# Scores of a linear-attention chunk: 64-key blocks on the two halves of TensorE, masked by four VectorE instructions instead of one

## The chip, the cores and the metric

The kernel runs on one core of one Trainium2 chip. Times are device microseconds of one execution. A run of a kernel consists of several executions, and the median is given; beside it stands one execution that the hardware profiler recorded, with a time and a span of its own.

## The reference

An attention layer with a complex decay per channel is followed by a gated feed-forward layer. Batch 4, 8 heads, 768 tokens, head dimension 48:

```python
for t in range(S):
    new_re = ar * S_re - ai * S_im
    new_im = ar * S_im + ai * S_re
    kv = np.einsum('bhd,bhe->bhde', k[:, :, t], v[:, :, t])
    S_re, S_im = (new_re + kv, new_im)
    y[:, :, t] = np.einsum('bhd,bhde->bhe', q[:, :, t], S_re)
...
a = x @ w_a
b = x @ w_b
return (a * b @ w_out)
```

`ar` and `ai` are the decay of token t, with its magnitude limited to 0.999; x is y with the heads side by side (384 columns); the feed-forward layer is 1536 wide. All of it is float32.

## The kernel before

The 768 tokens are cut into six chunks of 128. A *unit* is one chunk of two batches; there are 12 units, 0 to 11, in two runs of six (units 0 to 5 for the first two batches, 6 to 11 for the others). Within a chunk the recurrence is written as attention: with P the running product of decays, the queries are multiplied by P and the keys divided by P, real and imaginary parts are stacked to 96 rows, and the output of a token is the sum over the keys of its chunk that are not later than itself, plus what the state from earlier chunks gives.

Four kinds of work run beside each other:

- `prep(u)`: VectorE and ScalarE compute the products P of a unit and multiply queries and keys in place in the tile `qk`. Much of it is VectorE work on 128x768 elements.
- `stack(u)`: DMAs issued on SP copy each head's 96 rows from `qk` into the tile `stk` (128 rows, the last 32 are zero; per head 256 query columns, 256 key columns).
- `attn(u)`: the attention of the unit, 18 pieces (12 in the last chunk of a run). `scores` multiplies keys by queries: for a batch i and four heads `hg`, four matmuls of 128 keys by 128 queries fill one PSUM buffer (`pm`, two of these), and one VectorE instruction multiplies it by a 0/1 mask (a query sees only keys that are not later) into the SBUF tile `am` (two copies, one per `hg`). `transposes` turns the keys around, through a `pm` buffer too; `outputs` multiplies `am` by the values and, from the second chunk on, the queries by the state, on four 32-column strips of TensorE (`tile_position=(0, qd * 32)`) into the tile `xp`; `state` updates the state.
- `gemm1(f)` and `gemm2(f)`: the feed-forward layer of the unit before in 12 slices f. Operands are split into a high and a low part, so each product is three matmuls. `gemm1` leaves its result in a PSUM buffer `ab` (three of these), ScalarE and VectorE turn it into `hh` and `hl`, and `gemm2` runs two slices later (`LAG`).

In the steady state (the loop over `w`), while the feed-forward of unit w runs, the pieces of `attn(w+1)` are put between its slices (from slice 5 or 6 on), VectorE works at `prep(w+3)` in portions between slices, and `stack(w+2)` follows at slice 10 or 11. The order of instructions on each engine is made by a planner from the program's order, priorities and its own costs: `high_priority` puts the feed-forward's evacuation (`MOE_FIRST`, 4000) ahead of the attention's (`ATTN_FIRST`, 2000), and that ahead of `prep`. On the chip each engine then goes through its own list in order. Where a matmul has no `tile_position`, it uses the whole 128x128 array.

The lines that matter below: 385 (the matmuls of the scores), 388 (the mask), 396 (transposes), 425 (outputs), 442 (state), 486 and 504 (the two products of the feed-forward), 494 to 497 (their evacuation).

Of the kernel before, what the change touches and what calls it, by code (L numbers as in the profile page):

```python
# [8 lines left out]
F32 = mybir.dt.float32  # L9
# [5 lines left out]
ALU = mybir.AluOpType  # L15
# [15 lines left out]
NG = NB // RUNS  # L31
# [25 lines left out]
ATTN_FIRST = 2000  # L57
# [4 lines left out]
def view(ap, offset, dims):  # L62
    return bass.AP(tensor=ap.tensor, offset=ap.offset + offset, ap=[list(ap.ap[0])] + dims)


def at_(i):
    return i // 2 * 2 * NB + i % 2
# [3 lines left out]
def tile_kernel(ctx: ExitStack, tc: tile.TileContext, a_d, qk_d, v_d, w_d, qn_d, kn_d, vn_d, an_d, out_d):  # L71
    nc = tc.nc
    vec, act, pe, sync = nc.vector, nc.scalar, nc.tensor, nc.sync

    const = ctx.enter_context(tc.tile_pool(name="const", bufs=1))
# [4 lines left out]
    small = fast.enter_context(tc.tile_pool(name="small", bufs=2))  # L80
    vpool = fast.enter_context(tc.tile_pool(name="vpool", bufs=2))
    kvp = fast.enter_context(tc.tile_pool(name="kvp", bufs=2))
# [6 lines left out]

    ident = const.tile([128, 128], F32, name="ident")  # L90
    make_identity(nc, ident)
    mask = const.tile([128, 128], F32, name="mask")
    nc.gpsimd.memset(mask, 1.0)
    nc.gpsimd.affine_select(out=mask, in_=mask, pattern=[[1, 128]], compare_op=ALU.is_ge,
                            fill=0.0, base=0, channel_multiplier=-1)
    biases = const.tile([128, 6], F32, name="biases")
    b_tiny, b_sq, b_eps, b_one, b_inv, b_rsq = (biases[:, i:i + 1] for i in range(6))
    vec.memset(b_tiny, TINY)
# [10 lines left out]
    stk = const.tile([128, H, RUN], F32, name="stk")  # L109
# [93 lines left out]
    def prep(u):  # L203
# [9 lines left out]
        for k in (1, 0):  # L213
            vec.tensor_tensor(out=view(zz, (1 + k) * W, PAIRS), in0=a_t[:, k].rearrange("p (b i e) -> p b i e", e=2, i=SUB // 2),
                              in1=sc.rearrange("p (b i e) -> p b i e", e=2, i=SUB // 2), op=ALU.mult)
# [7 lines left out]
        def tok(s, i, o, n):  # L223
            return zb[:, s, i // 2, o:o + n, i % 2]

        parts = [(p * NB // 2, NB // 2) for p in range(2)] if u == 0 else [(0, NB)]
        for i in range(1, SUB):
            pr = small.tile([128, 2, 2, NB], F32, name="pr", bufs=1)
            for o, n in parts:
                vec.tensor_tensor(  # L230
                    out=pr[:, :, :, o:o + n],
                    in0=view(zz, W + at_(i) + 2 * o, [[W, 2], [-W, 2], [2, n]]),
                    in1=tok(slice(1, 3), i - 1, o, n).unsqueeze(1).broadcast_to([128, 2, 2, n]),
                    op=ALU.mult)
            for o, n in parts:
                vec.tensor_tensor(out=tok(slice(1, 3), i, o, n), in0=pr[:, :, 0, o:o + n],  # L236
                                  in1=pr[:, :, 1, o:o + n], op=ALU.add)
# [18 lines left out]
        cc, bb = c_t[:], b_t[:]  # L256

        def joined(out, x, y, n):
            pb = small.tile([128, 2, 2, NG], F32, name="pb")
            vec.tensor_tensor(out=pb[:, :, :, 0:n], in0=x,  # L260
                              in1=y.unsqueeze(1).broadcast_to([128, 2, 2, n]), op=ALU.mult)
            vec.tensor_tensor(out=out, in0=pb[:, :, 0, 0:n], in1=pb[:, :, 1, 0:n], op=ALU.add)

        vec.tensor_copy(out=c_t[:, 1:3, 0], in_=view(zz, W + at_(SUB - 1), [[W, 2], [2 * RUNS, NG]]))
        for k in range(1, RUNS):
            joined(c_t[:, 1:3, k], view(zz, W + at_(SUB - 1) + 2 * k, [[W, 2], [-W, 2], [2 * RUNS, NG]]),
                   c_t[:, 1:3, k - 1], NG)
        vec.tensor_scalar(out=c_t[:, 0], in0=c_t[:, 2], scalar1=-1.0, scalar2=None, op0=ALU.mult)
        n_run = NSB // RUNS
        for k in range(n_run):  # L270
            dst = b_t[:, 1:3, :, (k + 1) * RUNS] if k + 1 < n_run else b8
            joined(dst, view(cc, NB + (RUNS - 1) * NG + k, [[NB, 2], [-NB, 2], [n_run, G]]), b_t[:, 1:3, :, k * RUNS], G)
        pr = small.tile([128, 2, 2, RUNS - 1, NG], F32, name="pr", bufs=1)
        for k in range(2):
            vec.tensor_tensor(out=pr[:, k], in0=view(cc, (1 + k) * NB, [[-NB, 2], [NG, RUNS - 1], [1, NG]]),
                              in1=view(bb, NB, [[NB, 2], [0, RUNS - 1], [RUNS, NG]]), op=ALU.mult)
        vec.tensor_tensor(out=view(bb, NB + 1, [[NB, 2], [1, RUNS - 1], [RUNS, NG]]),
                          in0=pr[:, :, 0], in1=pr[:, :, 1], op=ALU.add)
# [10 lines left out]
        for k in range(2):  # L289
            pz = a_t  # L290
            for s in range(2):
                vec.tensor_tensor(  # L292
                    out=pz[:, s].rearrange("p (j b e) -> p j b e", j=SUB // 2, e=2), in0=zb[:, 1 + s],
                    in1=view(bb, (1 + k - s) * NB, [[0, SUB // 2], [1, NB], [0, 2]]), op=ALU.mult)
# [3 lines left out]
                              in0=view(pz[:], 0, PAIRS), in1=view(pz[:], W, PAIRS), op=ALU.add)  # L298
            yield 870
        act.activation(out=a_t, in_=z[:, 0:2], func=AF.Square)  # L300
        if rescaled(c):
            vec.tensor_tensor(out=bn[:, 1:3, :, 0], in0=b8,
                              in1=rho[:].unsqueeze(1).broadcast_to([128, 2, G]), op=ALU.mult)
# [67 lines left out]
    def attn(u, xh, xl):  # L371
# [3 lines left out]
        ams, kts, xps = {}, {}, {}  # L375

        def cols(i):
            return slice(i * C, (i + 1) * C), slice(TOK + i * C, TOK + (i + 1) * C)

        def scores(i, hg):  # L380
            qs, ks = cols(i)
            sp = ps_m.tile([128, 4, 128], F32, name="pm")
            for h4 in range(4):
                h = hg * 4 + h4
                pe.matmul(out=sp[:, h4], lhsT=stk[:, h, ks], rhs=stk[:, h, qs], start=True, stop=True)  # L385
            am = kvp.tile([128, 512], F32, name="am", bufs=2).rearrange("p (h t) -> p h t", h=4)
            with tc.high_priority(offset=ATTN_FIRST):
                vec.tensor_tensor(out=am, in0=sp, in1=mask[:].unsqueeze(1).broadcast_to([128, 4, 128]),  # L388
                                  op=ALU.mult)
            ams[i, hg] = am  # L390

        def transposes(i, hg):
            qs, ks = cols(i)
# [42 lines left out]
        def state(i, hg):  # L436
# [10 lines left out]
            with tc.high_priority(offset=ATTN_FIRST):  # L447
# [4 lines left out]
                if rescaled(c):  # L452
                    vec.tensor_tensor(out=uv, in0=uv, in1=sv, op=ALU.mult)

        order = [(scores, 0, 0), (scores, 0, 1), (transposes, 0, 0), (transposes, 0, 1),
                 (outputs, 0, 0), (outputs, 0, 1), (scores, 1, 0), (residual, 0, 0), (state, 0, 0), (scores, 1, 1),
                 (state, 0, 1), (transposes, 1, 0), (transposes, 1, 1), (outputs, 1, 0),
                 (outputs, 1, 1), (state, 1, 0), (residual, 1, 0), (state, 1, 1)]
        if u == 0:
            order = [(scores, 0, 0), (scores, 0, 1), (outputs, 0, 0), (outputs, 0, 1), (scores, 1, 0), (scores, 1, 1),  # L460
                     (residual, 0, 0), (outputs, 1, 0), (outputs, 1, 1), (transposes, 0, 0), (transposes, 0, 1),
                     (residual, 1, 0), (state, 0, 0), (state, 0, 1), (transposes, 1, 0), (transposes, 1, 1),
                     (state, 1, 0), (state, 1, 1)]
        for fn, i, g in order:
            if not (last and fn in (transposes, state)):
                fn(i, g)
                yield

    def pieces(u):
        return 12 if u % NCH + 1 == NCH else 18  # L470
# [161 lines left out]
    for _ in attn(0, *x_cur):  # L632
        drain(p1, P1_A)
# [13 lines left out]
    for w in range(NU):  # L647
        last = w + 1 == NU
        x_nxt = None if last else new_x()
        at = None if last else attn(w + 1, *x_nxt)  # L650
        if not last:
            load_v(w + 1)
# [13 lines left out]
        for f in range(NF):  # L666
            if w == 0:
                next(ws, None)
                drain(p1, P1_F)
                if f == P1_AT:  # L670
                    drain(p1)
                    stack(1)
                    for i in range(WARM):
                        wp = ps_m.tile([128, 512], F32, name="pm")
                        pe.matmul(out=wp[:, 0:TOK], lhsT=ident, rhs=qk[:, i % NJ, 1 - i // NJ % 2, TOK:2 * TOK],
                                  start=True, stop=True)
# [87 lines left out]
```

## Time and profile before

| | us |
|---|---|
| median of 3 runs | 698.79 (698.2 to 699.16) |
| profiled execution | 698.89 |
| its span | 697.2 |
| TensorE busy (matmuls) | 655.2, 5854 records |
| VectorE busy | 551.8, 1241 instructions |
| ScalarE busy | 308.9 |
| score matmuls, line 385 | 54.4 busy, 384 records |
| mask, line 388 | 32.8 busy, 48 instructions |

Matmul records overlap, since their ends are modelled: the mean duration of a record is not the time that it takes from its successors. A float32 matmul has two records, a matmul of the split feed-forward operands one. The chain of work that ended last, in order of time, merges neighbours of one line into one row (start, length, engine, tile, line, how many), and there the length of a row is what it took of the time.

### The profile page before, as it was taken

To read this page: it belongs to the slowest core of one execution; us is meant where nothing else is said; L and a number is where in the kernel's file an instruction comes from. 1 tells how busy PE (TensorE), PEld (TensorE's weight loads), DVE (VectorE), ACT (ScalarE), POOL (GpSimd) and SP (SyncE) were. 2 spreads that over 40 slices of the span, in tenths; PEclk is the share of its full clock that TensorE was granted. 3 is DMA by queue.
4 is the path that set the end of the run, shared out by engine and by line. 5 is a ranking of instruction groups with operands and counts; after the bars stand their busy time and mean duration, and the time that the engine had idled before them with its cause. 6 is when DMAs were issued, how large, how long until landed. Compare 5 with 4: busy or idle time off the path is not lost.

```text
span 697.2 us, 14316 instructions
## 1 busy us (share of the span) xinstructions
PE 655.2 (94%) x5854; PEld 610.8 (88%) x5854; DVE 551.8 (79%) x1241; ACT 308.9 (44%) x618; POOL 5.6 (1%) x11
## 2 busy tenths in 40 slices
PE   3557999999999999999999999999999999999996
PEld 1224889899899999999999999999999999999996
DVE  5999899988888889989899898999989853232221
ACT  6357755634535445245363554535542332221221
POOL 3000000000000000000000000000000000000000
PEclk9567999999999999999999999999999999999999
DMA  8973202411414205134151340511510500400000
GB/s 312 402 291 108 79 1 54 129 55 55 128 42 130 81 28 149 60 98 129 25 160 46 102 134 1 169 67 47 145 46 2 165 25 17 106 24 2 24 1 28
DMA packets 32088, 63.94 MB, mean 92 GB/s; under 512 B 3984, under 2 KB 10640, under 8 KB 32016
## 3 DMA queue, kind: packets, MB, share of 16 engines
q1 hardware_dynamic: 28560, 58.23, 27.0%
q10 hardware_dynamic: 3456, 4.72, 1.9%
q8 instruction: 48, 0.79, 0.5%
q14 instruction: 24, 0.20, 0.1%
HBM read 39.32 MB, written 4.72 MB: 63 GB/s over the span
## 4 chain that ended last, share of the span: by engine, by line
PE 64%; DVE 27%; ACT 4%; DMA 2%; issue 1%; SPq 1%; ACTq 0%; DVEq 0%
PE ab L486 30%; PE o L504 14%; PE xp L425 6%; PE pm L385 5%; PE pm L442 4%; DVE a_t L292 3%; DVE pr L230 2%; DVE qk L312 2%; DVE h_t L495 2%; PE pm L396 2%; DVE hl L497 2%; PE pm L150 2%; DVE z L297 2%; DVE pb L260 1%; DVE z L236 1%
## 5 line engine op out<-in xcount | busy, mean ns | idle before, releaser
L486 PE MATMUL ab<-xh,w 128*128 128x256 f32 x1728 | 339.0, 285 | 0.0
L486 PEld LDWEIGHTS ab<-xh,w 128*128 128x128 f32 x1728 | 278.1, 190 | 1.8 <-issue 1.4
L486 PE MATMUL ab<-xl,w 128*128 128x256 f32 x864 | 245.1, 284 | 0.0
L486 PEld LDWEIGHTS ab<-xl,w 128*128 128x128 f32 x864 | 164.4, 190 | 0.5 <-issue 0.2
L504 PE MATMUL o<-w,hh 128*128 128x384 f32 x576 | 152.3, 344 | 0.0
L494 ACT COPY h_t<-ab 128x256 f32<-128x256 f32 x144 | 53.1, 369 | 176.9 <-PE ab L486 176.8
L495 DVE TENSOR_TENSOR h_t<-ab,h_t 128x256 f32<-128x256 f32 x144 | 60.5, 420 | 72.5 <-ACT h_t L494 72.3
L504 PEld LDWEIGHTS o<-w,hh 128*128 128x128 f32 x576 | 96.8, 190 | 3.7 <-issue 3.0
L504 PE MATMUL o<-w,hl 128*128 128x384 f32 x288 | 96.9, 336 | 0.0
L496 ACT CAST hh<-h_t 128x256 fp32r<-128x256 f32 x144 | 58.0, 403 | 81.1 <-DVE h_t L495 80.9
L497 DVE TENSOR_TENSOR hl<-h_t,hh 128x256 fp32r<-128x256 f32 x144 | 60.5, 420 | 17.5 <-ACT hh L496 17.3
L150 PE MATMUL ab<-o_sb,ident 128*128 128x384 f32 x42 | 29.1, 794 | 29.9 <-DVE o_sb L141 29.8
L385 PE MATMUL pm<-stk 128*128 128x128 f32 x384 | 54.4, 279 | 2.7 <-DMA stk<-qk 2.7
L504 PEld LDWEIGHTS o<-w,hl 128*128 128x128 f32 x288 | 54.1, 188 | 0.0
L385 PEld LDWEIGHTS pm<-stk 128*128 128x128 f32 x384 | 48.7, 191 | 5.9 <-issue 4.8
L230 DVE TENSOR_TENSOR pr<-z 128x384 f32<-128x384 f32 (+1 forms) x91 | 47.1, 524 | 2.4 <-ACT z L216 0.8
L150 PEld LDWEIGHTS ab<-o_sb,ident 128*128 128x128 f32 x42 | 10.2, 286 | 39.8 <-DVE o_sb L141 29.4
L292 DVE TENSOR_TENSOR a_t<-z,b_t 128x768 f32<-128x768 f32 x48 | 44.6, 952 | 0.1
L425 PE MATMUL xp<-am,v_t 128*32 128x128 f32 x768 | 42.5, 277 | 1.3 <-DVE am L388 1.2
L312 DVE TENSOR_TENSOR qk<-qk,z 128x1536 f32<-128x1536 f32 (+1 forms) x28 | 42.7, 1524 | 0.1
L388 DVE TENSOR_TENSOR am<-pm,mask 128x512 f32<-128x512 f32 x48 | 32.8, 685 | 5.0 <-PE pm L385 4.8
L425 PE MATMUL xp<-stk,u 128*32 128x128 f32 x640 | 34.4, 273 | 0.0
(106 smaller groups left out, 761.7 us busy)
## 6 DMA issues: line engine op xcount, KB each, us to landing
w<-in_dram SPq DMA_DIRECT2D x36, 384.0 KB, 8.1
qk<-in_dram SPq DMA_DIRECT2D x12, 768.0 KB, 4.8
a_t<-in_dram SPq DMA_DIRECT2D x11, 768.0 KB, 4.3
stk<-qk SPq DMA_DIRECT2D x42, 192.0 KB, 3.3
v_t<-in_dram SPq DMA_DIRECT2D x24, 256.0 KB, 2.7
out_dram<-o_sb ACTq DMA_DIRECT2D x24, 192.0 KB, 1.9
stk<-qk SPq DMA_DIRECT2D x18, 192.8 KB, 3.4
stk<-qk SPq DMA_DIRECT2D x14, 128.0 KB, 3.1
```

Source lines behind the costliest of these rows:

```text
L150: pe.matmul(out=lp[:, 0:n], lhsT=ident, rhs=t, start=True, stop=False)
L230: vec.tensor_tensor(out=pr[:, :, :, o:o + n], in0=view(zz, W + at_(i) + 2 * o, [[W, 2], [-W, 2], [2, n]]), in1=tok(slice(1, 3), i - 1, o, ...
L292: vec.tensor_tensor(out=pz[:, s].rearrange("p (j b e) -> p j b e", j=SUB // 2, e=2), in0=zb[:, 1 + s], in1=view(bb, (1 + k - s) * NB, [[0, ...
L312: vec.tensor_tensor(out=qk4[:, :, k, x0:x1], in0=qk4[:, :, 1, x0:x1], in1=z[:, k].rearrange("p (j t) -> p j t", j=NJ).unsqueeze(2).broadca ...
L385: pe.matmul(out=sp[:, h4], lhsT=stk[:, h, ks], rhs=stk[:, h, qs], start=True, stop=True)
L425: pe.matmul(out=xp[qd * 32:(qd + 1) * 32, ti], lhsT=l, rhs=rr, start=st, stop=sp_, tile_position=(0, qd * 32), skip_group_check=True)
L486: pe.matmul(out=ab[:, m * TOK:(m + 1) * TOK], lhsT=r(w_ab(f, part, m * NJ + i)), rhs=r(xt[:, i, :]), start=n == 0, stop=n == 8)
L494: act.copy(out=h_t, in_=ab[:, 0:TOK])
L495: vec.tensor_tensor(out=h_t, in0=ab[:, TOK:2 * TOK], in1=h_t, op=ALU.mult)
L496: act.copy(out=r(hh), in_=h_t)
L497: vec.tensor_tensor(out=r(hl), in0=h_t, in1=hh, op=ALU.subtract)
L504: pe.matmul(out=os_[tt][:, 0:DM], lhsT=r(ht[:, ts]), rhs=r(w_t[f, 2][:, part, :]), start=(f == 0 and n == 0), stop=(f == NF - 1 and n == 2))
```

## The change

Unit 0 keeps its scores as they were. From unit 1 on a head's 128 keys are taken in two blocks of 64. Block 0 meets all 128 queries, block 1 only the queries 64 to 127, so the block of late keys and early queries (all masked) isn't computed. A block uses 64 columns of TensorE and writes 64 partitions of the PSUM buffer. For an even head block 0 goes to the lower half and block 1 to the upper; for an odd head the other way round, so that a pair of heads has 192 query columns on either half. VectorE's masking puts the odd heads' halves back: it reads one half of the partitions and writes the other, with a second mask for them. It is four instructions: even heads, lower half, queries 0 to 63; odd heads' block 0, 128 queries, from the upper to the lower half; odd heads' block 1 from the lower to the upper half; and even heads, all partitions, queries 64 to 127.

The masked tiles become two constant tiles. Their block that is no longer written (keys 64 to 127, queries 0 to 63) is zeroed once by GpSimd at the end of unit 0. The mask tile holds two masks and is made by three selects instead of one. To make room, the tile `pb` of `prep` has one buffer instead of two.

```diff
-    mask = const.tile([128, 128], F32, name="mask")
+    mask = const.tile([128, 2, 128], F32, name="mask")
     nc.gpsimd.memset(mask, 1.0)
-    nc.gpsimd.affine_select(out=mask, in_=mask, pattern=[[1, 128]], compare_op=ALU.is_ge,
-                            fill=0.0, base=0, channel_multiplier=-1)
+    for rows, base in ((mask[:, 0], 0), (mask[:, 1], 64), (mask[0:64, 1], -64)):
+        nc.gpsimd.affine_select(out=rows, in_=rows, pattern=[[1, 128]], compare_op=ALU.is_ge,
+                                fill=0.0, base=base, channel_multiplier=-1)
+    am2 = [const.tile([128, 4, 128], F32, name=f"am{hg}") for hg in range(2)]
...
-            pb = small.tile([128, 2, 2, NG], F32, name="pb")
+            pb = small.tile([128, 2, 2, NG], F32, name="pb", bufs=1)
...
             sp = ps_m.tile([128, 4, 128], F32, name="pm")
-            for h4 in range(4):
-                h = hg * 4 + h4
-                pe.matmul(out=sp[:, h4], lhsT=stk[:, h, ks], rhs=stk[:, h, qs], start=True, stop=True)
-            am = kvp.tile([128, 512], F32, name="am", bufs=2).rearrange("p (h t) -> p h t", h=4)
+            am = ams[i, hg] = am2[hg]
+            if u == 0:
+                for h4 in range(4):
+                    h = hg * 4 + h4
+                    pe.matmul(out=sp[:, h4], lhsT=stk[:, h, ks], rhs=stk[:, h, qs], start=True, stop=True)
+                with tc.high_priority(offset=ATTN_FIRST):
+                    vec.tensor_tensor(out=am, in0=sp, in1=mask[:, 0:1].broadcast_to([128, 4, 128]), op=ALU.mult)
+                return
+            for h4 in (0, 2):
+                for b in range(2):
+                    for x in range(2):
+                        h, g = hg * 4 + h4 + x, b ^ x
+                        pe.matmul(out=sp[64 * g:64 * (g + 1), h4 + x, 64 * b:],
+                                  lhsT=stk[:, h, ks.start + 64 * b:ks.start + 64 * (b + 1)],
+                                  rhs=stk[:, h, qs.start + 64 * b:qs.stop], start=True, stop=True,
+                                  tile_position=(0, 64 * g), skip_group_check=True)
             with tc.high_priority(offset=ATTN_FIRST):
-                vec.tensor_tensor(out=am, in0=sp, in1=mask[:].unsqueeze(1).broadcast_to([128, 4, 128]),
-                                  op=ALU.mult)
-            ams[i, hg] = am
+                for to, at, x, t0, t1 in ((0, 0, 0, 0, 64), (0, 64, 1, 0, 128), (64, 0, 1, 64, 128)):
+                    vec.tensor_tensor(out=am[to:to + 64, x::2, t0:t1], in0=sp[at:at + 64, x::2, t0:t1],
+                                      in1=mask[at:at + 64, x:x + 1, t0:t1].broadcast_to([64, 2, t1 - t0]), op=ALU.mult)
+                vec.tensor_tensor(out=am[:, 0::2, 64:], in0=sp[:, 0::2, 64:],
+                                  in1=mask[:, 0:1, 64:].broadcast_to([128, 2, 64]), op=ALU.mult)
...
+        if u == 0:
+            for am in am2:
+                nc.gpsimd.memset(am[64:128, :, 0:64], 0.0)
```

## The prediction

> **What bounds the kernel now.** I read the page first (busy shares and the shares of the chain that ended last), then windows of 45 to 50 us, then the groups by form, and last the chain itself in order of time, because the change touches one small group (the 384 records of line 385) and everything hangs on what stands around it.
>
> ```profile
> span 697.2 us, 14316 instructions
> ...
> PE 655.2 (94%) x5854; PEld 610.8 (88%) x5854; DVE 551.8 (79%) x1241; ACT 308.9 (44%) x618; POOL 5.6 (1%) x11
> ...
> PE 64%; DVE 27%; ACT 4%; DMA 2%; issue 1%; SPq 1%; ACTq 0%; DVEq 0%
> ```
>
> ```profile
> 180.00:230.00 50.00, 48.99 (x481) 45.51 (x480) 43.71 (x98) 24.59 (x47) 0.00 (x0) 1.00 0.29 85
> ...
> 475.00:525.00 50.00, 49.61 (x489) 48.04 (x488) 45.84 (x94) 23.99 (x46) 0.00 (x0) 1.00 0.28 83
> ...
> 576.00:627.00 51.00, 51.00 (x502) 49.85 (x501) 15.39 (x36) 12.90 (x33) 0.00 (x0) 1.00 0.18 50
> ```
>
> The columns of the windows are length, PE, PEld, DVE, ACT and POOL busy, granted clock, DMA share, GB/s. TensorE is never out of work from 130 us on, and its clock is fully granted. VectorE is busy 44 to 46 of 50 us until about 570 us and only then has time (15 of 51). So TensorE's work is the bound, and VectorE is a close second for units 1 to 9: the chain is 27% VectorE although TensorE hardly stops. A change that trades TensorE time for VectorE time has to be priced on both.
>
> **The parts, and what each costs.** First what the scores are today, and the nearest rows for what they become.
>
> ```profile
> L385 PE MATMUL pm<-stk 128*128 128x128 f32 x384 | 54.4, 279 | 2.7 <-DMA stk<-qk 2.7
> L425 PE MATMUL xp<-am,v_t 128*32 128x128 f32 x768 | 42.5, 277 | 1.3 <-DVE am L388 1.2
> L442 PE MATMUL pm<-v_t,kt 128*96 128x48 f32 x320 | 32.6, 245 | 0.0
> ...
> L388 DVE TENSOR_TENSOR am<-pm,mask 128x512 f32<-128x512 f32 x48 | 32.8, 685 | 5.0 <-PE pm L385 4.8
> L495 DVE TENSOR_TENSOR h_t<-ab,h_t 128x256 f32<-128x256 f32 x144 | 60.5, 420 | 72.5 <-ACT h_t L494 72.3
> ```
>
> A float32 matmul leaves two records, so a call of scores (four heads) is 8 records. Durations overlap (279 ns each), so the pace must come from the chain, here in unit 7:
>
> ```profile
> 423.21 0.60 DVE am L388
> ...
> 424.13 0.61 DVE am L388
> ...
> 424.79 0.55 PE pm L396 x4
> 425.34 2.17 PE ab L486 x18
> 427.51 1.89 PE xp L425 x64
> 429.40 1.27 PE o L504 x6
> 430.66 0.89 PE pm L385 x8
> 431.56 2.15 PE ab L486 x18
> 433.70 0.64 PE pm L442 x8
> 434.34 0.96 PE pm L385 x8
> 435.30 1.05 PE o L504 x6
> ...
> 439.89 1.01 PE xp L425 x32
> 440.90 1.25 PE o L504 x6
> ```
>
> *Streaming.* A call takes 0.89 us, 111 ns a record, and costs its neighbours nothing: 18 records of line 486 behind it take the same 2.15 us as elsewhere. The new call has per pair of heads two blocks of 128 queries and two of 64, one of each in either 64-column half of the array. That two halves can work at once is seen on line 425, where four 32-column strips do:
>
> ```profile
> 427.44 0.32 PE L425 MATMUL xp<-am,v_t 128*32 128x128 f32 x4
> ```
>
> Four records of 277 ns end within 0.32 us, and 64 of them take 1.89 us, 29.5 ns each against 111. If halves behave like strips, a call is per half four records of 111 ns and four of about 56 (half the queries): 0.67 us, a saving of 0.22. Bounds: a record of 64 queries may be no faster than the 48-query ones of line 442 (0.64 / 8 = 80 ns), then 0.76 us and a saving of 0.13; if halves took turns, 8 x 111 + 8 x 56 = 1.34 us, a loss of 0.45. I take 0.22, since line 425 is the only row with part of the array. For 44 calls (units 1 to 11) that is 9.7 us at most.
>
> *Entering and leaving the split array.* The same rows show a price that the score calls of today don't pay. 64 records of line 425 take 1.89 us but 32 take 1.01, where 32 more cost 0.88: 0.13 us is spent per visit on entering. And the six records of line 504 behind such a visit take 1.25 or 1.27 us, against 1.05 behind whole-array work: 0.20 or more on leaving. A visit to the split array costs 0.33 us whatever is done in it. The new scores are split too, so each stretch of line 385 becomes such a visit. In units 4 to 11 a unit has three on the chain, one with two calls and two with one:
>
> ```profile
> 372.27 1.78 PE pm L385 x16
> ```
>
> That gives per unit 3 x 0.33 - 4 x 0.22 = +0.11 us, 0.9 over the eight units. In units 1 to 3 the calls are in pieces, as heads arrive; units 2 and 3:
>
> ```profile
> 175.66 0.46 PE pm L385 x2
> ...
> 181.43 0.42 PE pm L385 x2
> ...
> 184.66 0.67 PE pm L385 x4
> ...
> 186.76 0.64 PE pm L385 x4
> ...
> 189.22 0.89 PE pm L385 x8
> ...
> 223.08 0.46 PE pm L385 x2
> ...
> 236.72 0.89 PE pm L385 x8
> ```
>
> From 175.66 to 189.22 there are 11 stretches, from 223.08 to 236.72 again 11, in unit 1 (129 to 138 us) five. One that borders line 425 on one side adds half a visit, on both sides none (a border is there already): 8.5, 9 and 4.5 visits more, 22 x 0.33 = 7.3 us. A stretch of two records is one head, whose two blocks go to different halves: 0.22 us, as today. Only whole pairs save: about 0.8 us in unit 1, 0.5 in each of units 2 and 3. Net +5.5. Bounds: if entering and leaving were free for halves, -9.7 in all; if the pieces were drawn together into three visits a unit, 11 x 0.11 = +1.2.
>
> The borders between line 425 and the new scores go from 32-column to 64-column work, which no row shows; I count them as drains. On this the Trainium skill, TensorEngine Tiling, section Tiling Modes, says that a change of tiling mode, not of tile, drains TensorE. The trace agrees for whole to strips (the 0.33 us); by that rule the borders stay as I count them, without it the ten such borders would save ten times half of 0.33 us, 1.7 in all.
>
> *Masking.* One VectorE instruction of 512 elements (685 ns) becomes four with 128, 256, 128 and 128. From lines 388 and 495 an element costs (685 - 420) / 256 = 1.04 ns, so 128 of them 288 ns. Whole durations: 3 x 288 + 420 = 1284 ns, 0.60 more a call; with 20 ns issue between them up to 0.66. If they overlap as today's do (0.60 of 685 ns counts in the chain, 85 ns less each), 0.34 more. I take 0.50, about the middle, since no row has two VectorE instructions that start on different partitions; that is 2.0 us a unit on an engine with 4 to 6 free. The Trainium skill, VectorE: DVE Perf Modes, section Two Vector instructions with no wait between them, says that one whose operand starts in another quadrant than the one before is held until all earlier ones have finished. Three of the four would be; the sum then goes by 0.66. No run so far shows it.
>
> Where does it count? On the chain the mask stands in front of TensorE at these places, beside the two at 423 us:
>
> ```profile
> 326.44 0.60 DVE am L388
> ...
> 327.37 0.60 DVE am L388
> ...
> 334.49 0.52 DVE am L388
> ...
> 338.69 0.61 DVE am L388
> ...
> 474.96 1.21 DVE am L388 x2
> ```
>
> Eight calls: 8 x 0.50 = +4.0 us (2.7 to 5.3). At 424.79 TensorE's transposes wait for it, because they need the PSUM buffer that the mask frees (two buffers), and behind them line 486. The other 36 calls lie where the chain is on TensorE; VectorE's free time hides 28 of them, and from 576 us the eight of units 10 and 11 cost nothing. If that cover were gone, 28 x 0.50 = 14 us more would be late, first VectorE's work for the unit after next, then its copies into the stacked tile, then scores.
>
> *The rest.* Two more selects and a wider fill on POOL at the start come out of an engine busy 5.6 us in all; the first masks are wanted after 60 us. The two zero fills at the end of unit 0 stand on POOL, which has nothing else, and unit 1's outputs come 60 us later. The pb tile with one buffer is written and read by VectorE in turn anyway, in order, and the masked tile keeps its two copies. All four at nothing; if the fills delayed VectorE, about 0.5 us each (two fills of 128x512 on POOL took 1.0).
>
> **Sum.** +0.9 (units 4 to 11) +5.5 (units 1 to 3) +4.0 (mask) = +10.4 us. The profiled execution took 698.89 us (697.2 of span), beside a median of 698.79: 709.3, rounded 709.
>
> **Rivals.** *Free switching* (faster): if 64-column halves need no drain, TensorE gains 9.7 us, and the mask gives 4.0 back, 693. For: TensorE is the bound, and line 385 runs at full density. Against: both sides of every visit to line 425 show the drain. *Pieces drawn together*: the order on TensorE is made anew with the new instructions; three visits a unit throughout give +1.2 + 4.0 = 704. For: units 4 to 11 already look so. Against: heads still arrive one by one. *VectorE becomes the bound* (slower): with 0.66 a call it gains 2.6 us a unit on 4 to 6 free, some of which are waits for ScalarE. If in units 1 to 9 nothing hides it, 36 x 0.66 = 24, with TensorE's loss hidden under it: 723. It decides once VectorE's free time in a window of 50 us is below one. *Halves take turns*: 44 x 0.45 = +20, 46 visits (22 and 3 in each of eight units) at 0.33 +15, mask +4: 738. Against: line 425.
>
> **How the numbers follow.** Forecast 0.50, own range 704 to 716 (mask 0.34 to 0.66, 64-query records 56 to 80 ns: 44 x 0.09 = 4 us). Free switching 0.20, pieces together 0.18, VectorE bound 0.08, turns 0.04. The range 692 to 718 leaves out the last two and little else. A difference under 0.2% (1.4 us) can't be told from none. Faster: 0.20, from free switching; same 0.06, where drawn-together pieces meet a mask that is hidden; slower 0.74.
>
> **What would show it.** Right: behind scores the six records of line 504 take 1.25 us, not 1.05; a lone call takes about 0.8 us with entry, not 0.89; VectorE's mask is four instructions that sum to 1.2 us or more; units 2 and 3 are longer by 2 us each. Wrong: no longer neighbours (free switching), 1.3 us a call (turns), or a chain that is mostly VectorE between 130 and 570 us (VectorE bound).

## The result, and the profile after

The changed kernel takes 730.98 us (median of four runs, 730.4 to 732.96), the kernel before 698.50 beside it: a ratio of 1.047, 95% interval 1.0447 to 1.0493. That is 32 us slower where 10 were forecast, and outside the range.

The page of the changed kernel (busy shares, then the shares of the chain), and two of its windows (columns as in the prediction):

```profile
span 729.7 us, 15169 instructions
...
PE 682.5 (94%) x6206; PEld 614.9 (84%) x6206; DVE 579.0 (79%) x1373; ACT 310.4 (43%) x618; POOL 7.1 (1%) x15
...
PE 67%; DVE 21%; DMA 4%; ACT 4%; issue 1%; SPq 1%; DVEq 0%; ACTq 0%
```

```profile
430.00:480.00 50.00, 49.35 (x484) 44.60 (x483) 42.05 (x101) 19.39 (x38) 0.00 (x0) 1.00 0.28 83
480.00:530.00 50.00, 50.00 (x501) 45.99 (x500) 42.55 (x99) 22.03 (x43) 0.00 (x0) 1.00 0.28 82
```

VectorE has 27 us more work (579.0 against 551.8), but in a window of 50 us between 180 and 530 us it is *less* busy than before (40 to 44 against 44 to 46). So it waits more. The shares of the chain tell little: DMA rose from 2 to 4%, VectorE's share fell from 27 to 21%. The groups say on what each engine waits:

```profile
L397 PE MATMUL pm<-stk 128*64 128x128 f32 x352 | 49.2, 289 | 7.9 <-DMA stk<-qk 7.9
...
L397 PE MATMUL pm<-stk 128*64 128x64 f32 x352 | 33.6, 225 | 0.0
```

```profile
L403 DVE TENSOR_TENSOR am<-pm,mask 64x128 f32<-64x128 f32 x88 | 24.8, 282 | 26.0 <-PE pm L397 25.2
...
L403 DVE TENSOR_TENSOR am<-pm,mask 64x256 f32<-64x256 f32 x44 | 18.7, 426 | 1.1 <-PE xp L441 0.4
```

Before, VectorE stood 4.8 us at the mask and waited for scores; now 25.2 us (the first of these two rows holds the two masks of 128 elements that use 64 partitions, the second the one of 256). TensorE stood 2.7 us for the copies into the stacked tile, now 7.9. Where this comes from is seen on the chain. In unit 7, whose scores came in three stretches before (line 385 at 421, 430.66 and 434.34 us), it is now:

```profile
439.73 3.37 DMA stk<-qk
443.10 0.14 issue
443.24 0.40 PE pm L397 x2
443.64 0.72 PE o L524 x3
444.36 0.48 PE pm L397 x5
444.84 0.72 PE o L524 x3
445.56 0.83 PE ab L506 x7
446.39 0.36 PE pm L397 x2
446.75 0.79 PE ab L506 x5
447.54 0.48 PE pm L397 x5
448.02 0.79 PE ab L506 x5
448.81 0.36 PE pm L397 x2
...
451.50 0.55 PE xp L441 x10
452.06 0.36 PE pm L397 x2
452.42 0.34 PE xp L441 x4
```

The scores start when a copy lands, and come head by head: two records for the first head of a pair, then the other six of the pair (a record is missing from the rows of five), with a few feed-forward matmuls between. Counting the stretches of score matmuls by their order in the trace gives 94 (60 before, of which six belong to unit 0 in either). Units 2 to 7 have 8 to 11 each, and only units 10 and 11 the three on which the prediction counted from unit 4 on. A call of scores is thus spread over 5 us (443.24 to 448). The mask behind it on VectorE, which has its list in a fixed order, holds up everything after it; that this is `prep` of a later unit, and so that unit's copies, is the reading that the experiments test.

The outputs (line 441, on strips) come in more pieces too: 65 stretches against 46. Counted over all TensorE records, the work changes between whole array, strips and halves 280 times; before it was 92 times. A visit has two such changes of mode, so one costs about half of 0.33 us.

The single prices on TensorE are as predicted. In unit 10, where the calls come whole:

```profile
605.80 1.59 PE pm L397 x31
607.39 1.26 PE o L524 x6
...
615.04 0.82 PE pm L397 x16
615.86 2.34 PE ab L506 x18
```

A call takes 0.82 us with entering (0.80 predicted), the group behind it 0.2 us more (1.26 against 1.05, 2.34 against 2.15). Per call that is 0.82 + 0.20 - 0.89 = +0.13, for two calls together 1.59 + 0.21 - 1.78 = +0.02, so +0.28 a unit where +0.11 was worked out. Going from 64-column to 32-column work costs a drain too, as the prediction counted it: from the last record of line 397 to the first of line 441 behind it, or the other way round, the median is 0.20 us (10 and 16 places in the trace), the same as from the strips to the whole array, while records within a stretch mostly start 0.01 to 0.11 us apart.

### The profile page after: what moved, and what is told of

It reads as the page before. It is cut to its first block, busy times and chain, and to the rows that moved or that the text cites. A ratio compares the mean times of both kernels' runs of the same rounds, so it can differ in the third digit from the quotient of the medians.

```text
span 729.7 us, 15169 instructions
## 1 busy us (share of the span) xinstructions
PE 682.5 (94%) x6206; PEld 614.9 (84%) x6206; DVE 579.0 (79%) x1373; ACT 310.4 (43%) x618; POOL 7.1 (1%) x15
## 4 chain that ended last, share of the span: by engine, by line
PE 67%; DVE 21%; DMA 4%; ACT 4%; issue 1%; SPq 1%; DVEq 0%; ACTq 0%
PE ab L506 29%; PE o L524 14%; PE xp L441 7%; PE pm L397 7%; PE pm L458 4%; DMA stk<-qk 4%; DVE qk L314 4%; DVE a_t L294 3%; PE pm L412 2%; DVE h_t L515 2%; PE pm L152 2%; DVE hl L517 2%; DVE z L299 1%; PE ab L152 1%; ACT a_t L302 1%
## 5 line engine op out<-in xcount | busy, mean ns | idle before, releaser
L403 DVE TENSOR_TENSOR am<-pm,mask 64x128 f32<-64x128 f32 x132 | 43.5, 330 | 27.1 <-PE pm L397 25.2
L397 PE MATMUL pm<-stk 128*64 128x128 f32 (+1 forms) x704 | 55.6, 257 | 7.9 <-DMA stk<-qk 7.9
L397 PEld LDWEIGHTS pm<-stk 128*64 128x64 f32 x704 | 40.3, 136 | 23.7 <-issue 15.0
L441 PE MATMUL xp<-am,v_t 128*32 128x128 f32 x768 | 48.4, 278 | 0.8 <-DVE am L391 0.6
L441 PE MATMUL xp<-stk,u 128*32 128x128 f32 x640 | 38.9, 275 | 0.0
```

The costliest lines, as they stand in the source:

```text
L397: pe.matmul(out=sp[64 * g:64 * (g + 1), h4 + x, 64 * b:], lhsT=stk[:, h, ks.start + 64 * b:ks.start + 64 * (b + 1)], rhs=stk[:, h, qs.star ...
L441: pe.matmul(out=xp[qd * 32:(qd + 1) * 32, ti], lhsT=l, rhs=rr, start=st, stop=sp_, tile_position=(0, qd * 32), skip_group_check=True)
```

## The experiments

All times are medians; the kernel before ran beside each of them on the same chip (699.37, 699.01, 698.75 and 698.84 us in the four series). Three theories: **T**, TensorE's visits to the split array cost the 32 us; **V**, VectorE's longer masks do; **L**, a loop, in which longer masks make the copies late, late copies bring the scores in pieces, and pieces cost visits and make VectorE wait.

### The parts alone

*Four masks behind whole-array scores* (`e1_mask4_whole`):

```diff
-            for h4 in (0, 2):
-                for b in range(2):
-                    for x in range(2):
...
+            for h4 in range(4):
+                h = hg * 4 + h4
+                pe.matmul(out=sp[:, h4], lhsT=stk[:, h, ks], rhs=stk[:, h, qs], start=True, stop=True)
```

> The changed kernel's four masking instructions behind whole-array scores as before (the exchange isn't made by the matmuls, so odd heads' rows come out in the wrong place). Theory V (VectorE: 0.64 us more per call, and waits at the masks, make it the bound of each unit): 718 to 730 us, TensorE waiting for the copies into the stacked tile in most units. Theory T (TensorE: visits to the split array cost it): only what the mask costs, 703 us at most.

713.11 us, ratio 1.0193 (1.0164 to 1.0223), +13.7. That lies between the two expectations: less than V's, and more than T's. There are 83 stretches of scores, which cost TensorE no drain here; but the outputs come in 60 stretches instead of 46, and these do (14 x 0.33 = 5 us, an estimate).

*Halves with one mask* (`e2_halves_mask1`), from the kernel before:

```diff
-                pe.matmul(out=sp[:, h4], lhsT=stk[:, h, ks], rhs=stk[:, h, qs], start=True, stop=True)
...
+                for g in range(2):
+                    pe.matmul(out=sp[64 * g:64 * (g + 1), h4], lhsT=stk[:, h, ks.start + 64 * g:ks.start + 64 * (g + 1)],
+                              rhs=stk[:, h, qs], start=True, stop=True, tile_position=(0, 64 * g), skip_group_check=True)
```

> The kernel before with scores on the two halves of TensorE (64 keys each, all 128 queries, no block skipped, no exchange) and its one masking instruction. Nothing is saved in streaming, so each visit costs its 0.33 us. Theory V: at most the 46 added visits of the prediction, 700 to 714 us, VectorE as before. Theory T: 720 to 730 us, about the whole loss.

711.00 us, ratio 1.0163 (1.0134 to 1.0193), +11.6, with 58 stretches. T alone falls: without a longer mask, the scores come in no more pieces than before, and their visits cost no more than the prediction's count times its price gives (46 added x 0.33 = 15 at most). Since nothing is skipped here, the changed kernel would take up to 9.7 us less. So the two parts alone make at most 13.7 + 11.6 = 25.3, and with the streaming saved about 16, of 32.

### VectorE's side

*Less VectorE work, in both kernels* (`e3_after_less_dve`, `e6_before_less_dve`):

```diff
-        vec.tensor_tensor(out=a_t[:, 0], in0=a_t[:, 0], in1=a_t[:, 1], op=ALU.mult)
...
-        vec.scalar_tensor_tensor(out=a_t[:, 0], in0=a_t[:, 0], scalar=2.0, in1=a_t[:, 1],
-                                 op0=ALU.subtract, op1=ALU.mult, reverse0=True)
...
-        vec.tensor_tensor(out=kk, in0=kk, in1=a_t[:, 0].rearrange("p (j t) -> p j t", j=NJ), op=ALU.mult)
+        vec.tensor_tensor(out=kk, in0=kk, in1=a_t[:, 1].rearrange("p (j t) -> p j t", j=NJ), op=ALU.mult)
```

> The changed kernel with two VectorE instructions of 0.96 us per unit left out (the refinement of the reciprocal, so the result is a little less exact). Theory V: 1.9 us or more per unit over some nine units come back, 705 to 715 us. Theory T: 728 to 731 us.

> The kernel before with the same two VectorE instructions of 0.96 us per unit left out as from the changed one (no refinement of the reciprocal, a little less exact). Theory L: the kernel before stands in the loop only in units 2 and 3, so little comes back, 692 to 698 us. Theory V in its plain form (each us on VectorE is a us of time): 9 to 12 units of 1.9 us, 675 to 684 us.

The changed kernel falls to 709.85 (ratio 1.0147, 1.0117 to 1.0176): 21 us for two instructions that sum to 1.9 us in each of 12 units (23 us). The kernel before falls by 2 us only (696.99; ratio 0.9979, 0.9959 to 0.9999) for the same 23. So a microsecond on VectorE has no fixed price in time. What differs is the pieces: the relieved kernel has 56 stretches instead of 94, three a unit from unit 5 on.

*More VectorE work in the kernel before, for which nothing waits* (`e4_before_more_dve`):

```diff
+                for _ in range(2 if u else 0):
+                    vec.tensor_tensor(out=mask, in0=mask, in1=mask, op=ALU.mult)
```

> The kernel before with two more VectorE instructions of 0.3 us behind each mask (the mask tile times itself), for which nothing waits. Theory V, if busy time alone decides: 715 to 725 us. Theory V, if the waits at the masks and the later scores decide: 700 to 707 us. Theory T: 699 to 701 us.

704.26 us, ratio 1.007 (1.0047 to 1.0093), +4.9, and 73 stretches. VectorE is busy 18.5 us longer than before (570.3), in `e1_mask4_whole` 26.2 us (578.0): two thirds of the busy time cost a third of the 13.7 us. That the rest comes from what waits for the masks is likely, but not shown.

*Four masks that start on one partition* (`e7_mask4_same_start`):

```diff
-                for to, at, x, t0, t1 in ((0, 0, 0, 0, 64), (0, 64, 1, 0, 128), (64, 0, 1, 64, 128)):
-                    vec.tensor_tensor(out=am[to:to + 64, x::2, t0:t1], in0=sp[at:at + 64, x::2, t0:t1],
...
+                for to, x in ((0, 0), (1, 0)):
+                    vec.tensor_tensor(out=am[0:64, to::2, 0:64], in0=sp[0:64, x::2, 0:64],
+                                      in1=mask[0:64, 0:1, 0:64].broadcast_to([64, 2, 64]), op=ALU.mult)
+                vec.tensor_tensor(out=am[:, 1::2, 64:], in0=sp[:, 1::2, 64:],
+                                  in1=mask[:, 1:2, 64:].broadcast_to([128, 2, 64]), op=ALU.mult)
```

> The changed kernel with four masking instructions of 128 elements that all start on partition 0 (odd heads get other scores than theirs), the matmuls unchanged. If an instruction that starts on other partitions than the one before it can't overlap with it, the four now take about 0.80 us of VectorE instead of 1.24. Theory L: close to the kernel in which VectorE was relieved by 1.9 us a unit, 708 to 718 us. Theory T (TensorE's visits alone): 728 to 731 us.

What the masks cost on VectorE stands in the timelines (start, length, line, shape, how many), first of the changed kernel, then of this one:

```profile
454.03 1.02 DVE L403 TENSOR_TENSOR am<-pm,mask 64x128 f32<-64x128 f32 x3 [1.62 <-PE pm L397]
455.09 0.29 DVE L405 TENSOR_TENSOR am<-pm,mask 128x128 f32<-128x128 f32 x1
455.30 0.95 DVE L191 TENSOR_TENSOR a_t<-a_t 128x768 f32<-128x768 f32 x1
```

```profile
451.17 0.48 DVE L403 TENSOR_TENSOR am<-pm,mask 64x128 f32<-64x128 f32 x2 [1.34 <-PE pm L397]
451.58 0.27 DVE L405 TENSOR_TENSOR am<-pm,mask 128x128 f32<-128x128 f32 x1
451.78 0.27 DVE L407 TENSOR_TENSOR am<-pm,mask 128x128 f32<-128x128 f32 x1
451.98 0.94 DVE L191 TENSOR_TENSOR a_t<-a_t 128x768 f32<-128x768 f32 x1
```

From the first mask to the next instruction it is 1.27 us against 0.81: where all start on partition 0 they follow each other every 0.20 us although each takes 0.27; in the changed kernel each starts 14 to 31 ns after the end of the one before. With 0.60 for the single mask, the change costs 0.67 us a call: the upper bound of the prediction (0.66). The four of the changed kernel also have 128 elements more. The Trainium skill, VectorE: DVE Perf Modes, section Two Vector instructions with no wait between them, gives this as its rule for a change of quadrant, and the trace agrees. The time lies between the two expectations: 723.54 (ratio 1.0344, 1.0311 to 1.0378), only 7.5 us better, still with 87 stretches. A relief of 0.46 us a call (1.8 us a unit) doesn't draw the pieces together, while 1.9 us a unit in `prep`, ahead of the copies, did. Why the place matters is not shown.

### The pieces

*A call in one stretch* (`e5_call_in_one`), the changed kernel with only the order of its matmuls bound:

```diff
-            for h4 in (0, 2):
-                for b in range(2):
-                    for x in range(2):
...
+            first = block(2, 0, 1)
+            with tc.issue_after(first.ins):
+                for h4, b, x in ((2, 0, 0), (2, 1, 0), (2, 1, 1), (0, 0, 0), (0, 0, 1), (0, 1, 0), (0, 1, 1)):
+                    block(h4, b, x)
```

> The changed kernel, where the matmuls of a call of scores are queued behind the one of its last head, so that a call isn't taken apart as its heads arrive. Theory L (a loop: longer masks make the copies late, late copies make the scores come in pieces, pieces cost TensorE a visit each and make VectorE wait at the masks, which makes the next copies late): with about half the visits 708 to 720 us, VectorE's waits at the masks well under the 25 us of the changed kernel. Theory V (VectorE's masking time alone): 725 to 731 us, since the masks are as long as before.

704.47 us, ratio 1.0084 (1.005 to 1.0118): 26.5 of the 32 us are gone, with the same matmuls and the same four masks, more than L expected. Its chain in unit 7, and VectorE's wait at the mask (25.2 us in the changed kernel):

```profile
425.68 0.82 PE pm L395 x16
...
430.13 0.89 PE pm L395 x16
...
434.71 0.82 PE pm L395 x16
...
438.24 0.82 PE pm L395 x16
```

```profile
DVE am L406 <- PE pm L395: 2.9, 6, 0.8
```

Three to five stretches a unit, 48 in all, and 183 changes of mode instead of 280. At half of 0.33 us each the 97 fewer changes are 16 of the 26.5 us, and TensorE's waits for copies are 5 less (2.9 instead of 7.9). This shows that the pieces are the cause, and V falls as an explanation of the whole. Most of the price is paid as visits, as in T, but it takes the longer masks to bring the pieces about.

*Only pairs held together* (`e13_pair_in_one`): the same, with `first = block(h4, 0, 1)` for each pair, so that a call may come in two stretches but no pair is broken.

> The changed kernel, where only the two heads of a pair are held together (the pair's matmuls queued behind the one of its second head), so that no pair is broken but a call can still come in two stretches. If visits to the split array are what the pieces cost, by their number: 712 to 722 us with some 75 visits. If broken pairs and VectorE's waits at the masks are: 704 to 710 us, near the kernel with whole calls.

712.52 us, ratio 1.0199 (1.0177 to 1.0221), the low end of the first expectation, with 66 stretches; VectorE waits 6.2 us at the masks:

```profile
DVE am L407 <- PE pm L395: 6.2, 13, 1.1
```

So 18 more stretches than with whole calls cost 8 us (0.45 each, a little over a visit), and the broken pairs of the changed kernel another 18.5. Of the 18.5 about 11 us are changes of mode by their number (280 against 214, half of 0.33 each); the rest would be lost overlap of the halves and what follows from VectorE's 19 us more of waiting, which these runs don't divide.

*The scores one slice later* (`e8_scores_later`):

```diff
-ATTN_AT = (5, 6, 6, 6, 6)
+ATTN_AT = (5, 7, 7, 7, 7)
```

> The changed kernel with the pieces of the attention put one slice of the feed-forward later (slice 7 instead of 6 from unit 2 on), so that the copies have 3.2 us more. Theory L: no waits for the copies and scores in three visits from unit 4 or 5 on, 708 to 720 us. Theory V: the masks are as long as before, 725 to 735 us.

723.15 us, ratio 1.0339 (1.0309 to 1.0369), 82 stretches: the order is hardly another in units 2 to 6, and three a unit come only from unit 9 on. L's number was missed. The place in the program's order didn't bind the planner here; what an instruction must follow did.

### Whole calls, and what is left of the change

Three kernels with calls in one stretch: four masks behind whole-array scores, the kernel before with its one mask, and the changed kernel with both calls of a batch in one stretch (two visits a unit). The first two have this in place of the loop over the four heads (`one` is the matmul of one head):

```diff
+            first = one(3)
+            with tc.issue_after(first.ins):
+                for h4 in range(3):
+                    one(h4)
```

> Whole-array scores with the four masking instructions (odd heads' rows in the wrong place, as in the first experiment), but a call's matmuls queued behind the one of its last head. Theory L: the masks alone without pieces cost little, 699 to 705 us, against 713 in pieces. If the masks' length itself cost the 14 us: 710 to 715.

> The kernel before with a call's matmuls queued behind the one of its last head, one masking instruction. Theory L: units 2 and 3, the only ones in pieces, get shorter by up to 2 us each, 694 to 699 us. If calls in one stretch make TensorE wait longer for the copies: 699 to 703.

> The changed kernel with the two calls of a batch made into one stretch of 32 records, queued behind the last head: two visits to the split array per unit instead of four. By the visit's price, 2 x 11 x 0.33 = 7 us less than with four visits: 695 to 700 us, about the kernel before. If the two PSUM buffers, both taken by scores at once, hold up the transposes: 702 to 710.

Results: 707.69 (ratio 1.013, 1.0112 to 1.0148), 696.20 (0.9968, 0.9954 to 0.9981) and 699.98 (1.001, 0.9997 to 1.0023). Differences to the kernel before in us, by what is done and how the calls come:

| scores, masks | in pieces | a call in one stretch |
|---|---|---|
| whole array, one mask | 0 | -2.6 |
| whole array, four masks | +13.7 | +8.9 |
| halves, four masks | +32.5 | +5.5 |

The masks cost 11 to 14 us either way; the first kernel lies between its two expectations. The halves cost 19 us in pieces and seem to *save* 3 in one stretch, but the outputs explain most of that: they come in 61 stretches in the first kernel and 54 in `e5_call_in_one`, and 7 x 0.33 is 2.3 us. With 46 stretches of outputs in the kernel before and 42 in the second, their visits are also some 5 to 6 us of what the masks cost.

The second kernel is the fastest of all, 0.3% under the one before, because the scores of units 2 and 3 no longer stop for each head. From the start of one unit's feed-forward to the next it takes 52.9 and 51.5 us while they run, before 54.6 and 53.3. Its unit 2:

```profile
178.44 1.13 PE pm L390 x8
...
182.75 0.89 PE pm L390 x8
...
186.47 1.09 PE pm L390 x8
...
188.91 0.89 PE pm L390 x8
```

*Joining the two* (`e12_whole_then_split`): units 1 to 3 as in the second, the rest as in the third.

```diff
+SPLIT_FROM = 4
...
-            if u == 0:
+            if u < SPLIT_FROM:
...
```

> Units 1 to 3 with whole-array scores and one mask, a call queued behind its last head; from unit 4 on the halves, both calls of a batch in one stretch, four masks. By the traces of the two kernels that it joins: 270.5 us to the start of unit 4's scores (from the kernel with whole-array calls in one stretch) and 415 us from there (from the one with two calls in one), 685 to 692 us, faster than the kernel before. If VectorE's lead at unit 4 is what the later units live on and four masks use it up: 695 to 700.

697.74 us, ratio 0.9988 (0.9974 to 1.0002): no difference to the kernel before that can be told. From the start of one unit's scores to the next it takes 51.1 to 51.5 us in units 7 to 11, where the kernel before has 50.6 to 51.4. The 415 us taken from the other trace came from scores that were catching up: there the scores of units 4 to 11 follow each other 8 us faster in all than before, but the feed-forward of the same units starts no faster (346.7 us from unit 4 to unit 11, before 346.5, here 348.6). So they can't be added to a start that was already ahead. At two visits a unit the halves give no time back against the kernel before, masks included.

One part of the change was not tested alone: `pb` with one buffer. VectorE's instructions on `pb` take as long as before (12.1 against 12.0 us, and 9.5 in both) and wait no longer, so its own cost doesn't show; what it does to the planner's order stays open.

## Why the prediction was wrong, by its own steps

The sign was right, the size a third (10.4 of 32.5 us), and the sum failed in three places.

**"In units 4 to 11 a unit has three on the chain" failed, and carried the rest.** The count of stretches was read from the order of the kernel before, and the prediction allowed that the order is made anew only in the good direction (pieces drawn together). Even there it was short: unit 4 has six stretches in order of time, of which the chain shows two. With VectorE's longer masks units 4 to 8 went over to pieces like those of units 2 and 3 (8 to 11 a unit, unit 9 six). In place of the 51 stretches counted for units 1 to 11 there were 88, and the outputs came in 19 more. The prediction's 46 added visits make 184 changes of mode where 280 were measured; the 96 more are 16 us at half of 0.33 each (an estimate), most of the 22 us that the sum missed. TensorE's waits for copies, at nothing in the sum, grew by 5 us. The kernel with whole calls has 42 stretches there and took 704.5. That this is near the 704 of "pieces drawn together" is in part luck, since its masks cost more than the 4.0 of that sum.

**"A stretch of two records is one head [...] 0.22 us, as today" failed** in what follows from it. In the changed kernel's list the six other records of a pair stand behind its second head, so a broken pair spreads a call out and keeps VectorE waiting: 25.2 us at the masks against 4.8 before and 6.2 with whole pairs. Whole-array scores in 83 stretches (`e1_mask4_whole`) make it wait only 6.5 us. No step priced a wait at the masks.

**"Eight calls: 8 x 0.50 = +4.0 us" failed.** The masks measure +13.7 behind whole-array scores. The price of a call was taken too low (0.50, measured 0.67, the upper bound), but 8 x 0.67 = 5.4 explains little. What was wrong is "VectorE's free time hides 28 of them". From the start of unit 1's feed-forward to that of unit 9's, and during unit 9's, the windows show, first for the kernel before, then for `e9_mask4_whole_in_one`:

```profile
144.90:553.30 408.40, 404.47 (x3859) 390.96 (x3859) 371.35 (x821) 186.23 (x361) 0.00 (x0) 1.00 0.29 86
553.30:603.80 50.50, 50.50 (x497) 49.35 (x496) 22.78 (x44) 15.77 (x35) 0.00 (x0) 1.00 0.23 67
```

```profile
146.00:559.60 413.60, 410.08 (x3853) 392.39 (x3853) 371.51 (x872) 184.85 (x359) 0.00 (x0) 1.00 0.27 81
559.60:611.50 51.90, 51.18 (x498) 49.45 (x497) 46.48 (x105) 18.10 (x38) 0.00 (x0) 1.00 0.23 65
```

VectorE does the same 371 us of work in the first stretch with and without the longer masks, and is idle 37 and 42 us there. So its gaps of 4 to 6 us a unit hid none of the added work. What the masks added pushed `prep` back, out of the first stretch and into unit 9's, where VectorE had time (22.8 us busy, now 46.5). Of the 37 us before, 29 are waits of VectorE, 22 for ScalarE and 7 for TensorE. That the 14 us named as the price of a missing cover come near the 13.7 is luck: at 0.67 a call they would be 19, and the outputs' visits are 5 of the 13.7.

Right were the price of a visit (0.33), the pace of the halves (0.82 us a call with entering), the drain between 64- and 32-column work, and that the start and the zero fills cost nothing that shows (the first feed-forward begins at 75.4 us, before at 75.5). In time "halves take turns" (738, chance 0.04) and "VectorE becomes the bound" (723, chance 0.08) came nearest, 7 and 8 us off, but not in mechanism: a call takes 0.82 us and not 1.34, and VectorE is less busy in a window than before and waits for TensorE.

What isn't shown is why the planner takes the calls apart: its lists are fixed before the run, they change with VectorE's work, and an order bound by hand undoes it. That it reckons with copies landing one by one, late, is argued from where the pieces stand, and so is the way of the loop from the masks to the copies.

## What to carry to other kernels

When an instruction list is planned anew after a change, the count of anything that costs per occurrence (here visits to the split array) must not be taken from the old order: price the change at the worst order that the old trace shows anywhere, here units 2 and 3. Work that pays on entering and leaving should be bound together by hand before it is timed. And idle time of an engine with a fixed list need not be cover: where it is waits for other engines, as here, added work takes its place beside them and moves what follows.

## What the runs showed of the hardware

A visit to the split array costs about 0.33 us to enter and leave, for strips of 32 and halves of 64 columns, and from one to the other there are 0.20 us between the records, as from strips to the whole array. In halves a call streams 25% fewer columns, and the visit eats that: a lone call costs 0.13 us more than on the whole array (0.82 + 0.20 against 0.89), two together 0.02 more (1.59 + 0.21 against 1.78). Four VectorE instructions of 128 elements take 0.81 us when they start on the same partition, while four of 128, 256, 128 and 128 that change it take 1.27 us. And two VectorE instructions of 0.96 us, left out in each unit ahead of its copies, were worth 21 us in the kernel whose scores came in pieces, and 2 us in the one before.
